# The ending of a fused state-space and attention kernel: when all engines branch on a flag, and where the flag is made

## The chip, the cores and the metric

The kernel runs on one core of a Trainium2 chip. The metric is the device time of one execution in microseconds (us).

## The reference

The input is `A_x`, 2048 rows of 1024 numbers in bf16. Two results are computed from it and mixed by a gate:

```python
g = _sigmoid((x * gate_w).sum(-1, keepdims=True))
# a: a diagonal state-space model with complex states
h = Lam_bar[None, :] * h + Bu[:, t, :]            # for each of 2048 steps t
y = 2.0 * jnp.einsum("blp,dp->bld", hseq, Cmat).real + x * Dskip[None, None, :]
# b: attention with 32 heads of 32 columns
scores = jnp.einsum("bhqd,bhkd->bhqk", q, k) * (Dh ** -0.5)
p = _softmax(scores, axis=-1)
o = jnp.einsum("bhqk,bhkd->bhqd", p, v)           # then reshaped, @ wo
return g * a + (1 - g) * b
```

The output has 2048 rows of 1024 bf16 numbers.

## The kernel before

The program holds two complete versions of the computation. The fast one assumes that the sums of the softmax lie in a safe range. It counts, at its end, whether all of them did, and makes a flag of the count. If the flag is zero, the program is done. Otherwise the general version, whose code follows, computes everything again. With the inputs of this case the flag is zero.

The fast version's attention runs in 512 bursts; a burst is two blocks of 128 keys, four heads and 256 queries. In each, PE forms scores (L1625), ACT takes their exponential (L1644, L1641), and PE multiplies by the values (L1728). The projections, the state-space model and the output matrix fill the gaps in portions that a planner places. The output is made in 16 tiles of 128 rows; each tile is collected in a buffer in SBUF (`fin`, which shares its memory with `f_xT` and so bears that name in the profile) and stored by one DMA of 256 KB that SP issues (`st_out`, L1573).

A small scheduler, `Sched`, keeps one list of operations for each engine (`pe`, `act`, `dve`, `pool`, `sp`). It works out from declared reads and writes which semaphores an operation waits for. All engines run their lists in order. `force_signal` makes an operation raise its engine's semaphore though no other operation in the lists needs it.

The last two tiles, 14 and 15, are finished in `tail`. For each of them (index `r`) PE multiplies the last group of attention results by the last rows of `wo`, once for each half of the columns (L2023, two matmuls for each `r`, into banks `2 + r` and `4 + r`). The first half is then copied by ACT (L2032), the second half added up by DVE (L2036), and `st_out` stores the tile. DVE has meanwhile reduced the checks to one bit per partition, `badb` (L2017). A matmul with a single column adds these up in bank 7 (L2026), and DVE converts the sum to an integer in SBUF, `flag` (L2034). In the kernel before, that matmul stands between the matmuls of tile 14 and tile 15, and the conversion ahead of DVE's part of tile 14.

After its list each engine runs the code of `stream`. It waits for the flag's conversion (L2092), loads the flag into a register (L2094, TENSOR_LOAD in the profile) and branches on it (L2095, COMPARE_BRANCH). A location for a branch hint is marked some way ahead in each list (`MARK_AT` operations before its end) and tied to this branch. The block of all engines is closed by a DRAIN on each and a barrier by semaphores (they bear L2060 in the profile).

`final_waits` waits for the semaphores of the DMA lanes: with `late` False for all lanes but those of the last two DMAs, with `late` True for the lanes of the last two, the stores of tiles 14 and 15. In the kernel before SP alone calls it: with False ahead of the flag, with True behind the branch.

Of the kernel before, what the change touches and what calls it, by code (L numbers as in the profile page):

```python
# [960 lines left out]
class FastPath:  # L961
# [85 lines left out]
    def dve(self, fn, r, w, name=""):  # L1047
        return self.S.op("dve", fn, reads=r, writes=w, name=name)
# [927 lines left out]
    def tail(self):  # L1976

        S, ps, OT, wo, dve = self.S, self.ps, self.OT, self.wo, self.dve
        chk, rc, osum = self.chk, self.rc, self.osum
        z = self.ut[:, 1, 0:34]  # L1980
        dve(lambda e: e.memset(z, 0.0), [], ["z"] + [("ut", 1)])

        def check(u0, u1, s0, s1, c):

            ra = rc[:, u0:u1].rearrange("p u g -> p (u g)")
            t, z2 = self.ut[:, 0, 0:8 * (u1 - u0)], self.ut[:, 1, 128:128 + s1 - s0]
            rcs, oss = [("rc", u) for u in range(u0, u1)], [("os", u) for u in range(s0, s1)]
            dve(lambda e: e.tensor_scalar(t, ra, RC_MAX, None, ALU.is_le), rcs, [("ut", 0)])
            dve(lambda e: e.scalar_tensor_tensor(t, ra, RC_MIN, t, ALU.is_ge, ALU.mult, accum_out=chk[:, c:c + 1]), rcs + [("ut", 0)], [("ut", 0), ("chk", c)])
            dve(lambda e: e.scalar_tensor_tensor(z2, osum[:, s0:s1], 0.0, z[:, s0:s1], ALU.mult, ALU.is_equal, accum_out=chk[:, c + 1:c + 2]), oss + ["z"], ["z2", ("chk", c + 1)])  # L1990

        def preload(r):
            for n in range(2):
                S.op("pe", lambda e, r=r, n=n: e.matmul(ps[:, 2 + r, :], self.ident[:], self.hilo[2 * r][n], start=(n == 0), stop=False),
                     reads=["ident", ("hi", 2 * r), ("lo", 2 * r)], name="preload", writes=[("tb", 2 + r)] + ([("S", 1)] if r == n == 0 else []), **({} if r == n == 0 else dict(acc=[("S", 1)])))
        assert self.os_n == 32 and not self.bg2
        check(0, 63, 0, 32, 0)
        self.pv(4 * NBURST - 8, 4 * NBURST - 4)
        preload(0)
        self.pv(4 * NBURST - 4, 4 * NBURST - 2)  # L2000
        self.pv(4 * NBURST - 2, 4 * NBURST)
        preload(1)
        ov = ps[:, 6, 0:264].rearrange("p (a c) -> p a c", a=8)
        On = self.On[:, 1]
        dve(lambda e: e.reciprocal(rc[:, 63], ov[:, :, 32]), ["O"], [("rc", 63)], "rcp")
        for t in range(2):
            o = On[:, t].rearrange("p (h c) -> p h c", h=4)
            dve(lambda e, t=t, o=o: e.scalar_tensor_tensor(o, ov[:, 4 * t:4 * t + 4, 0:32], self.gcol[:, 1, 14 + t:15 + t],
                                                           rc[:, 63, 4 * t:4 * t + 4].unsqueeze(2).to_broadcast([128, 4, 32]), ALU.mult, ALU.mult,
                                                           accum_out=osum[:, 32 + t:33 + t]), ["O", ("rc", 63), "g1"], [("On", 1, t), ("os", 32 + t)], "norm")  # L2010
            S.op("pe", lambda e, t=t: e.matmul(ps[:, t, 0:128], On[:, t], self.ident[:], start=True, stop=True),
                 reads=[("On", 1, t), "ident"], name="xp", **(dict(writes=[("S", 0), ("xp", t)]) if t == 0 else dict(acc=[("S", 0)], writes=[("xp", t)])))
        for t in range(2):
            self.act(lambda e, t=t: e.activation(OT[:, 7, 1792 + 128 * t:1920 + 128 * t], ps[:, t, 0:128], ACT.Copy), [("xp", t)], [("OT", 7, 7, t)], "xp")
        check(63, 64, 32, 34, 2)
        dve(lambda e: e.tensor_reduce(chk[:, 4:5], chk[:, 0:4], AX.X, ALU.add), [("chk", c) for c in range(4)], [("chk", 4)])
        dve(lambda e: e.tensor_scalar(self.badb[:, 0:1], chk[:, 4:5], 545.5, None, ALU.is_lt), [("chk", 4)], ["badb"])  # L2017

        for r in range(2):
            for cb in range(2):  # L2020
                bank = 2 + r + 2 * cb
                w = dict(acc=[("tb", bank)]) if cb == 0 else dict(writes=[("tb", bank)] + ([("S", 2)] if r == 0 else []), **({} if r == 0 else dict(acc=[("S", 2)])))
                S.op("pe", lambda e, r=r, cb=cb, bank=bank: e.matmul(ps[:, bank, :], OT[:, 7, 1792 + 128 * r:1920 + 128 * r], wo[7][0][:, 512 * cb:512 * (cb + 1)],  # L2023
                                                                    start=(cb == 1), stop=True), reads=[("OT", 7, 7, r), "wo7"], name="tail", **w)
            if r == 0:
                S.op("pe", lambda e: e.matmul(ps[0:1, 7, 0:1], self.badb[:, 0:1], self.badb[:, 1:2], start=True, stop=True), reads=["badb", "one"],  # L2026
                     writes=[("bank", 7)], name="flag")
        for r in range(2):
            fb = self.fin_n % 8 // 2
            self.fin_n += 2  # L2030
            o = self.fin[fb]
            self.act(lambda e, o=o, r=r: e.activation(o[:, 0:512], ps[:, 2 + r, :], ACT.Copy), [("tb", 2 + r)], [("fin", fb, 0)], "evac_t")  # L2032
            if r == 0:
                self.flag_op = dve(lambda e: e.tensor_copy(self.flag[:], ps[0:1, 7, 0:1]), [("bank", 7)], ["flag"], "flag")  # L2034
                self.flag_op.force_signal = True
            dve(lambda e, o=o, r=r: e.scalar_tensor_tensor(o[:, 512:1024], ps[:, 4 + r, :], 1.0, self.sum7[2 * r + 1], ALU.mult, ALU.add),  # L2036
                [("tb", 4 + r), ("sum7", 2 * r + 1)], [("fin", fb, 1)], "evac_t")
            self.st_out(14 + r, fb)
def bass_gated_mix__ssm_conv_s5__mha_block__prompt_kernel(
    nc: bass.Bass,  # L2040
    A_x: bass.AP,
# [18 lines left out]
    with ExitStack() as es:  # L2060
        S = Sched(n_dma_lanes=15, own=1)
        S2 = Sched(n_dma_lanes=12, pool_in_order=True, serial_xpose=True)
        sems = {l: es.enter_context(nc.semaphore("f_" + l)) for l in S.lanes()}
        sems2 = {l: es.enter_context(nc.semaphore("g_" + l)) for l in S2.lanes()}
        go = es.enter_context(nc.semaphore("go"))
        flag = es.enter_context(nc.sbuf_tensor("flag", [1, 1], I32))
# [14 lines left out]
        def stream(name, e):  # L2081

            loc = []
            S.emit(name, e, sems, MARK_AT[name], lambda: loc.append(e.mark_branch_hint_location()))
            if not loc:
                loc.append(e.mark_branch_hint_location())
            if name == "pool":
                for _ in range(272):
                    e.nop()
            if name == "sp":  # L2090
                S.final_waits(e, sems, False)
            e.wait_ge(sems[fast.flag_op.lane], fast.flag_op.tick)  # L2092
            with e.register("bad_" + name) as r:
                e.reg_load(r, flag[0:1, 0:1])  # L2094
                br = e.br_cmp(r, 0, on_true="done_" + name, on_false="bad_" + name, comp_op="IS_EQ")  # L2095
                br.branch_hint(loc[0])
                with e.bass.body("bad_" + name):
                    if name == "sp":
                        S.final_waits(e, sems, True)
                        e.nop().then_inc(go, 1)  # L2100
                    e.wait_ge(go, 1)
                    S2.emit(name, e, sems2)
                    if name == "sp":
                        S2.final_waits(e, sems2)
                    e.br("done_" + name)
                e.bass.switch_bb("done_" + name)
            if name == "sp":
                S.final_waits(e, sems, True)

        @block.sync  # L2110
        def _(e):
            stream("sp", e)

        @block.tensor
        def _(e):
            stream("pe", e)

        @block.vector
        def _(e):
            stream("dve", e)  # L2120
# [36 lines left out]
```

## Time and profile before

| | |
|---|---|
| median of 3 runs | 925.74 us (924.91 to 925.8) |
| profiled execution | 925.63 us |
| its span, first to last instruction | 923.9 us |
| PE busy | 901.5 us (98%) |
| ACT busy | 905.7 us (98%) |
| DVE busy | 770.5 us (83%) |
| SP's stores of the output | 16, median 2.2 us from issue to landing |

Busy times are shares of the span. An engine's name with a q (SPq, DVEq) stands for its sequencer, whose instructions (waits, register loads, branches, the issue of DMAs) are not counted as busy. Of the DMA queues, q1 carries the data that SP and ACT ask for; q8 and q14 carry instructions, in packets of 16 KB and 8 KB. The median from issue to landing counts from the start of the issuing instruction to the last update of the DMA's semaphore. The ending that the change touches is the stretch from about 917 us to the end of the span.

### The profile page before, as it was taken

How to read it: one execution, taken by the hardware profiler on the slowest of the kernel's cores; microseconds unless marked ns; L12 is line 12 of the kernel's file. 1: busy time of each engine (PE TensorE's matmuls, PEld its weight loads, DVE VectorE, ACT ScalarE, POOL GpSimd, SP SyncE). 2: the span in 40 equal slices, each digit the busy share in tenths (PEclk: the TensorE clock that was granted, in tenths of full speed). 3: DMA queues.
4: the chain of work that ended last, by engine and by line, in shares of the span. 5: the costliest groups of instructions: out<-in, count | busy, mean ns of one | idle time of the engine just before them, and what ended most of it. 6: DMA issues, size and time to landing. Idle time of an engine off the chain costs nothing.

```text
span 923.9 us, 34036 instructions
## 1 busy us (share of the span) xinstructions
PE 901.5 (98%) x15316; PEld 503.1 (54%) x15316; DVE 770.5 (83%) x1345; ACT 905.7 (98%) x1034; POOL 86.4 (9%) x163
## 2 busy tenths in 40 slices
PE   8899999999999999999999999999999999999996
PEld 4555744556555565555655565555655655545553
DVE  2788989999989999999999999989998655676665
ACT  6999999999999999999999999999999999999996
POOL 2000001011000101010111110101001010000010
PEclk9999999999999999999999999999999999999999
DMA  9449767630564202242212621622001012534422
GB/s 199 86 101 150 105 116 146 139 83 16 104 118 100 65 20 72 75 97 53 41 41 77 127 50 25 133 65 67 20 22 48 21 60 69 185 85 129 114 62 75
DMA packets 170983, 77.70 MB, mean 84 GB/s; under 512 B 147280, under 2 KB 155472, under 8 KB 170832
## 3 DMA queue, kind: packets, MB, share of 16 engines
q1 hardware_dynamic: 168672, 74.94, 35.7%
q8 instruction: 121, 1.98, 0.9%
q10 hardware_dynamic: 2160, 0.53, 0.3%
q14 instruction: 30, 0.25, 0.1%
HBM read 25.18 MB, written 20.97 MB: 50 GB/s over the span
## 4 chain that ended last, share of the span: by engine, by line
PE 54%; ACT 36%; DVE 5%; SPq 1%; DMA 1%; issue 1%; POOL 0%; DVEq 0%
ACT f_pt L1644 29%; PE f_ps L1728 14%; PE f_ps L1625 11%; PE f_ps L1427 9%; PE f_ps L1505 8%; PE f_ps L1458 6%; PE f_ps L1446 5%; ACT f_pt L1641 5%; SPq L1063 1%; ACT f_cT L1644 1%; DVE f_ht L1363 1%; ACT f_Et L1644 1%; PE f_ps L1707 1%; DMA f_xT<-in_A_x_dram 1%; PE f_ps L1511 0%
## 5 line engine op out<-in xcount | busy, mean ns | idle before, releaser
L1644 ACT ACTIVATE f_pt<-f_ps 128x1024 bf16<-128x1024 f32 x746 | 718.2, 1086 | 2.7 <-PE f_ps L1625 2.3
L1728 PEld LDWEIGHTS f_ps<-f_V,f_pt 128*128 128x128 bf16 x7156 | 220.8, 96 | 96.1 <-issue 69.7
L1728 PE MATMUL f_ps<-f_V,f_pt 128*128 128x33 bf16 x7156 | 257.2, 178 | 0.6 <-ACT f_pt L1644 0.6
L1625 PE MATMUL f_ps<-f_Q,f_K 32*128 32x256 bf16 x4096 | 203.3, 273 | 9.0 <-ACT f_cT L1644 2.2
L1641 ACT ACTIVATE f_pt<-f_ps 128x768 bf16<-128x768 f32 x198 | 176.6, 892 | 0.0
L1625 PEld LDWEIGHTS f_ps<-f_Q,f_K 32*128 32x128 bf16 x4096 | 60.7, 92 | 146.8 <-ACT f_pt L1644 118.5
L1458 PE MATMUL f_ps<-f_xT,f_wb 128*128 128x512 bf16 x512 | 131.5, 379 | 1.3 <-DVE f_pf L1240 0.5
L1666 POOL TENSOR_SCALAR f_xp<-f_xq 128x512 int16<-128x512 f32 x99 | 66.9, 676 | 618.9 <-DVE f_xq L1665 418.5
L1427 PE MATMUL f_ps<-f_xT,f_wb 128*128 128x512 bf16 x464 | 119.3, 379 | 0.4 <-DVE f_Q L1434 0.3
L1634 DVE TENSOR_SCALAR f_xi<-f_ps 128x256 int32<-128x256 f32 x198 | 83.4, 421 | 15.9 <-PE f_ps L1625 11.6
L1363 DVE TENSOR_TENSOR_SCAN f_ht<-f_pf,f_init,f_ut 128x512 bf16<-128x512 f32 x64 | 81.1, 1279 | 0.0
L1505 PE MATMUL f_ps<-f_cT,f_hp 128*128 128x512 bf16 x272 | 74.5, 379 | 0.1
L1669 DVE SCALAR_TENSOR_TENSOR f_xq<-f_xq,f_xi 128x512 f32<-128x512 f32 x99 | 68.5, 692 | 3.3
L1668 DVE SCALAR_TENSOR_TENSOR f_xq<-f_xi 128x512 f32<-128x512 uint16 x99 | 68.5, 692 | 3.3
L1665 DVE SCALAR_TENSOR_TENSOR f_xq<-f_xi,f_xq 128x512 f32<-128x512 int16 x99 | 68.2, 689 | 2.2
L1458 PEld LDWEIGHTS f_ps<-f_xT,f_wb 128*128 128x128 bf16 x512 | 40.1, 96 | 40.3 <-issue 9.1
L1446 PE MATMUL f_ps<-f_wb,f_xT 128*128 128x128 bf16 x896 | 59.3, 219 | 0.0
L1427 PEld LDWEIGHTS f_ps<-f_xT,f_wb 128*128 128x128 bf16 x464 | 36.1, 96 | 35.9 <-issue 7.6
L1446 PEld LDWEIGHTS f_ps<-f_wb,f_xT 128*128 128x128 bf16 x896 | 50.4, 97 | 3.8 <-issue 3.8
L1462 DVE CAST f_ub<-f_ps 128x512 bf16<-128x512 f32 x64 | 44.0, 688 | 9.5 <-PE f_ps L1458 8.6
L1741 DVE RECIPROCAL f_rc<-f_ps 128x8 f32<-128x8 f32 x63 | 13.0, 207 | 40.0 <-PE f_ps L1707 34.5
L1536 PE MATMUL f_ps<-f_cT,f_OT 128*128 128x512 bf16 x156 | 44.7, 378 | 0.1
(149 smaller groups left out, 829.0 us busy)
## 6 DMA issues: line engine op xcount, KB each, us to landing
u_scratch<-f_ub SPq DMA_DIRECT2D x64, 128.0 KB, 2.0
f_ub<-u_scratch SPq DMA_DIRECT2D x32, 256.0 KB, 2.9
ag_scratch<-f_Ag SPq DMA_DIRECT2D x32, 256.0 KB, 2.2
f_hp<-ag_scratch SPq DMA_DIRECT2D x32, 256.0 KB, 3.0
f_wb<-in_B_wqkv_dram SPq DMA_DIRECT2D x21, 256.0 KB, 4.1
out_dram<-f_xT SPq DMA_DIRECT2D x16, 256.0 KB, 2.2
f_cT<-in_B_wo_dram SPq DMA_DIRECT2D x5, 256.0 KB, 5.5
f_OT<-f_On SPq DMA_TRANSPOSE x63, 2.5
```

What stands on the lines that cost most here:

```text
L1363: ops.append((1.2, 0.0, lambda ri=ri: dve(lambda e: e.tensor_tensor_scan(ht[:, ri, :], rr, ut[:, ri, :], self.init[:, ri, j:j + 1], ALU.mu ...
L1427: mms.append((1, lambda e, f, l, a=a, w=w: e.matmul(ps[:, bank, :], w[:, a, :], xT[:, a, 512 * ch:512 * (ch + 1)], start=f, stop=l), [tok] ...
L1446: m = e.matmul(ps[:, bank, 128 * q:128 * (q + 1)], xT[:, a, 128 * kt:128 * (kt + 1)], w[:, a, :], start=(a == 0), stop=(a == 7))
L1458: mms.append((1, lambda e, f, l, a=a: e.matmul(ps[:, 7, :], bT[:, (2 * n + ri) % 3, a, :], xT[:, a, 512 * ch:512 * (ch + 1)], start=f, sto ...
L1505: mms.append((1, lambda e, f, l, j=j, ri=ri, h=h: e.matmul(ps[:, 7, :], h[:, cols], cT[ri][:, j, 512 * cb:512 * (cb + 1)], start=f, stop=l ...
L1625: m = e.matmul(ps[:, 2 * sl[h // 2] + h % 2, 256 * kl:256 * (kl + 1)], K[32 * h:32 * h + 32, g % 2, 128 * kt:128 * (kt + 1)], Q[32 * h:32 ...
L1634: first = self.dve(lambda e: e.tensor_scalar(self.xi[:, b % 2, X_COLS * n:X_COLS * (n + 1)], ps[:, 2 * s + 1, 512 - X_COLS:512], X_A, X_LO ...
L1641: self.S.op("act", lambda e: e.activation(flat(self.tile[p]), flat(ps[:, 2 * s:2 * s + 2, :]), ACT.Exp, scale=SCALE), reads=[("S", s)], wr ...
L1644: self.act(lambda e: e.activation(self.tile[p], ps[:, 2 * s:2 * s + 2, :], ACT.Exp, scale=SCALE), [("S", s)], [("pt", p)], "exp")
L1668: return [(0.61, DEP, lambda: self.dve(lambda e: e.scalar_tensor_tensor(xq[:], lo, E2 / E3 * w, lo, ALU.add, ALU.mult), i2, ["xq"], "x_q") ...
L1669: (0.61, DEP, lambda: self.dve(lambda e: e.scalar_tensor_tensor(xq[:], xq[:], E1 / E3 * w * w, lo, ALU.add, ALU.mult), ["xq"] + i2, ["xq"] ...
L1728: m = e.matmul(ps[:, 6, o:o + 33], self.tile[p][:, h2, 256 * kl + 128 * qt:256 * kl + 128 * (qt + 1)], V[:, g % 2, 2 * i + kl, h, :], star ...
```

## The change

In `tail`, the flag's matmul moves behind all four matmuls of tiles 14 and 15, and its conversion on DVE moves behind both of DVE's evictions and the issue of both stores in program order. In `stream`, every engine now waits for the last two stores between the load of the flag and the branch; SP no longer does so after the branch, nor does the code of the general version.

```diff
@@ tail
-            if r == 0:
-                S.op("pe", lambda e: e.matmul(ps[0:1, 7, 0:1], self.badb[:, 0:1], self.badb[:, 1:2], start=True, stop=True), reads=["badb", "one"],
-                     writes=[("bank", 7)], name="flag")
+        S.op("pe", lambda e: e.matmul(ps[0:1, 7, 0:1], self.badb[:, 0:1], self.badb[:, 1:2], start=True, stop=True), reads=["badb", "one"],
+             writes=[("bank", 7)], name="flag")
         for r in range(2):
...
             self.act(lambda e, o=o, r=r: e.activation(o[:, 0:512], ps[:, 2 + r, :], ACT.Copy), [("tb", 2 + r)], [("fin", fb, 0)], "evac_t")
-            if r == 0:
-                self.flag_op = dve(lambda e: e.tensor_copy(self.flag[:], ps[0:1, 7, 0:1]), [("bank", 7)], ["flag"], "flag")
-                self.flag_op.force_signal = True
             dve(lambda e, o=o, r=r: e.scalar_tensor_tensor(o[:, 512:1024], ps[:, 4 + r, :], 1.0, self.sum7[2 * r + 1], ALU.mult, ALU.add),
                 [("tb", 4 + r), ("sum7", 2 * r + 1)], [("fin", fb, 1)], "evac_t")
             self.st_out(14 + r, fb)
+        self.flag_op = dve(lambda e: e.tensor_copy(self.flag[:], ps[0:1, 7, 0:1]), [("bank", 7)], ["flag"], "flag")
+        self.flag_op.force_signal = True
@@ stream
             e.wait_ge(sems[fast.flag_op.lane], fast.flag_op.tick)
             with e.register("bad_" + name) as r:
                 e.reg_load(r, flag[0:1, 0:1])
+                S.final_waits(e, sems, True)
                 br = e.br_cmp(r, 0, on_true="done_" + name, on_false="bad_" + name, comp_op="IS_EQ")
                 br.branch_hint(loc[0])
                 with e.bass.body("bad_" + name):
                     if name == "sp":
-                        S.final_waits(e, sems, True)
                         e.nop().then_inc(go, 1)
...
                 e.bass.switch_bb("done_" + name)
-            if name == "sp":
-                S.final_waits(e, sems, True)
```

## The prediction

> **What bounds the kernel now.** The change touches only what comes after the last evictions, so I read the page for the span and then only the last seven microseconds, in this order: the timeline, SP's waits, the DMA traffic by queue, and the lines of the branch and of the closing barrier.
>
> ```profile
> span 923.9 us, 34036 instructions
> ```
>
> The profiled execution took 925.63 us, so 1.73 us lie outside its span. The median of the three runs is 925.74 us, 0.11 above it; I make the sum against the profiled execution and add 0.11 at the end.
>
> The timeline of the ending (start, length, engine, line, operation):
>
> ```profile
> 916.40 0.55 ACT L2014 ACTIVATE f_OT<-f_ps 128x128 bf16<-128x128 f32 x2 [1.39 <-PE f_ps L2011]
> ...
> 916.74 0.61 PE L2023 MATMUL f_ps<-f_cT,f_OT 128*128 128x512 bf16 x2
> ...
> 916.95 0.16 DVE L2017 TENSOR_SCALAR f_badb<-f_chk 128x1 bf16<-128x1 f32 x1
> 917.16 1.23 ACT L2032 ACTIVATE f_xT<-f_ps 128x512 bf16<-128x512 f32 x2 [0.21 <-PE f_ps L2023]
> ...
> 917.27 0.17 PE L2026 MATMUL f_ps<-f_badb 128*1 128x1 bf16 x1
> ...
> 917.37 0.61 PE L2023 MATMUL f_ps<-f_cT,f_OT 128*128 128x512 bf16 x2
> 917.47 0.14 DVE L2034 CAST flag<-f_ps 1x1 int32<-1x1 f32 x1 [0.36 <-PE f_ps L2026]
> 917.55 1.27 DVE L2036 SCALAR_TENSOR_TENSOR f_xT<-f_ps,f_Et 128x512 bf16<-128x512 f32 x2
> ```
>
> SP's own timeline and its waits (engine and line, for what, us in total, times, longest):
>
> ```profile
> 918.30 0.92 SPq L1573 DMA_DIRECT2D out_dram<-f_xT  x2
> ...
> SPq L195 <- DMA out_dram<-f_xT: 2.3, 1, 2.3
> SPq L2060 <- DMA out_dram<-f_xT: 0.6, 1, 0.6
> ```
>
> The last computation ends at 917.55 + 1.27 = 918.82; the span ends at 923.9. The five microseconds between are SP alone, standing in front of the last two stores. So this ending is bounded by the landing of the stores, and the question is why that takes so long. The DMA view of 918 to 924 (queue: packets, MB, share of 16 engines; then the issue, KB, median us to landing), and below it the instruction queues' lines of three shorter windows, 919 to 920.2, 920.2 to 920.6 and 921.4 to 921.6:
>
> ```profile
> q1 hardware_dynamic: 288, 0.52, 26.2%
> q14 instruction: 4, 0.03, 2.2%
> q8 instruction: 1, 0.02, 1.0%
> ...
> out_dram<-f_xT SPq DMA_DIRECT2D x2, 256.0 KB, 4.6
> ...
> q14 instruction: 3, 0.02, 7.9%
> ...
> q8 instruction: 1, 0.02, 15.5%
> ...
> q14 instruction: 1, 0.01, 17.8%
> ```
>
> Both last stores need 4.6 us. The page's median over all 16 stores, the store of 907.4 (DMA view of 907 to 910, without an instruction queue in it), and the store of 872.9 (872.8 to 876.7, with one instruction packet in it):
>
> ```profile
> out_dram<-f_xT SPq DMA_DIRECT2D x16, 256.0 KB, 2.2
> ...
> q1 hardware_dynamic: 144, 0.26, 23.4%
> ...
> out_dram<-f_xT SPq DMA_DIRECT2D x1, 256.0 KB, 2.0
> ...
> q8 instruction: 1, 0.02, 2.3%
> ...
> out_dram<-f_xT SPq DMA_DIRECT2D x1, 256.0 KB, 3.7
> ```
>
> An undisturbed store lands in 2.0 to 2.2 us; one that shares its time with an instruction fetch takes 3.7; the last two share theirs with five fetches and take 4.6. Where the five fetches come from is read from the branch (L2095), the flag's loads into registers (L2094) and the closing barrier (L2060): duration in ns, then the start.
>
> ```profile
> L2094 DVEq TENSOR_LOAD <-flag x1: 546/546/546, 918.0 to 918.0; - x1
> L2094 SPq TENSOR_LOAD <-flag x1: 762/762/762, 919.6 to 919.6; - x1
> ...
> L2095 POOLq COMPARE_BRANCH  x1: 65/65/65, 918.2 to 918.2; - x1
> L2095 PEldq COMPARE_BRANCH  x1: 496/496/496, 918.2 to 918.2; - x1
> L2095 ACTq COMPARE_BRANCH  x1: 68/68/68, 918.3 to 918.3; - x1
> L2095 DVEq COMPARE_BRANCH  x1: 84/84/84, 918.6 to 918.6; - x1
> L2095 SPq COMPARE_BRANCH  x1: 78/78/78, 920.4 to 920.4; - x1
> ...
> L2060 POOLq DRAIN  x1: 125/125/125, 918.6 to 918.6; - x1
> L2060 PEldq DRAIN  x1: 58/58/58, 918.8 to 918.8; - x1
> L2060 ACTq DRAIN  x1: 78/78/78, 918.8 to 918.8; - x1
> L2060 DVEq DRAIN  x1: 34/34/34, 919.2 to 919.2; - x1
> L2060 SPq COMPARE_BRANCH  x1: 53/53/53, 923.5 to 923.5; - x1
> L2060 SPq DRAIN  x1: 13/13/13, 923.7 to 923.7; - x1
> ```
>
> Five engines branch and five instruction packets move: four branches between 918.2 and 918.6, four packets between 919 and 920.6; SP's branch at 920.4, and a lone packet in 921.4 to 921.6, some 1.1 us behind it. I take it that each taken branch makes its engine fetch more code, and that these fetches fall on the DMA engines that carry the stores issued at 918.30 and 918.89. No view shows the DMA engine of a packet, so the collision itself is inferred.
>
> **The change part by part.** *The flag leaves the head of the evictions.* The conversion at 917.47 stands ahead of the first DVE eviction, and waits for a matmul that waits for L2017's result. The bank that the eviction reads is done at 916.74 + 0.61 = 917.35. The DVE took up the flag 0.03 us after its matmul's end at 917.44; by the same step the eviction starts at 917.38 instead of 917.55, 0.17 earlier. The second follows: it starts 1.27 - 0.67 = 0.60 later, at 917.98 (0.67 being half of the pair's work, about 1.3 us). Its bank is ready before that: tile 15's operand is there at 916.40 + 0.55 = 916.95, matmuls of this kind follow at 0.61 - 0.38 = 0.23 us, and without the flag's matmul between them the second pair runs from 917.19 to 917.80. The ACT evictions, 917.16 to 918.39, end before the DVE's. So the DVE ends at 918.65 and the last store is issued at 918.72. Gain 0.17, bounds 0 and 0.2.
>
> *The flag itself.* It is now made after 918.65, so at about 918.82. Four engines then load it in some 0.55 us (the DVE's row) and are done at 919.4. SP gets there after its store: its load of 919.6 to 920.4 moves up by the 0.17 to end at 920.2. All this lies beside the stores. It would cost something only if they landed before 920.2, 1.5 us after the last issue, and none did so in under 2.0.
>
> *The waits for the stores, on all five engines.* Behind them on each engine stand the branch, the drain and the barrier, and nothing else; only the barrier waits for these. The waits cost nothing before the landing.
>
> *The fetches move behind the landing.* With every branch behind both stores, no branch-made fetch can disturb them. The landing goes from 4.6 to between 2.0 (alone, 907.4) and 2.4: the two stores are 0.59 us apart, and 0.52 MB in the way makes the second one queue a little. I take 2.2, the page's median: 918.72 + 2.2 = 920.92, against 918.89 + 4.6 = 923.5 before. If the fetches are not the cause, this gain of 2.4 is nil.
>
> *The branch is now exposed.* Before, SP alone came late and had only its jump left: 923.5 to the DRAIN's end at 923.7, 0.2 us. Now all five branch at 920.94. From the start of the branch to the end of the drain it was 0.5 us on POOL, 0.66 on PE, 0.58 on ACT and 0.63 on DVE. I take 0.65 for the latest, with 0.5 and 0.9 as bounds. That is a loss of 0.45. The barrier after it stays: 923.9 - 923.7 = 0.2.
>
> The sum: 920.94 + 0.65 + 0.2 = 921.8 for the span, against 923.9, or -0.17 - 2.4 + 0.45 = -2.1. With the 1.73 outside, 923.5; with 0.11 for the median, **923.6 us**, 0.23% less.
>
> **A rule that speaks against it.** The four drains start between 918.6 and 919.2, and four of the five fetches had not arrived by 919.2: the code behind the branch was already there, and the fetches were for later code. The Trainium skill, page "Runtime: NRT & Kernel Launch", section "Instruction fetch mechanics", says that a taken branch whose target is outside the two pages at hand stops its engine until that page has been fetched. Here the trace shows no such stop. Where the rule bites, the fetch would stand behind the landing on all five engines, which is the third rival below, at 926.4 us; by the row of the drains it does not, and the sum stays.
>
> **The rivals.** *The fetches become the tail.* The code fetched after the branch may be needed soon after the barrier, in the part outside the span. Today there are three microseconds of landing to hide it. SP's packet moved 1.1 us after its branch; PE's, branched at 918.2, moved from 920.2 to 920.6 at the earliest and took 1.0% of 16 engines' 6 us, about 1 us, so its code was there 3.0 to 3.4 us after the branch. From 920.94 that makes 922.6 (1.1, and half a microsecond for a packet of q14: 2.2% of 16 engines' 6 us, by four) to 924.3, and with the 0.2 and 1.73 a time of 924.5 to 926.2, likeliest 925.1. For it speaks that each engine did fetch; against it, that no drain or barrier waited for a fetch.
>
> *The stores land late for another reason.* Being two in a row, say. Then the landing stays 4.6: 918.72 + 4.6 + 0.65 + 0.2 = 924.2, so 925.9 to 926.0, no change. Against it speaks the single store at 872.9 with 3.7. Equivalent to it is that the fetches come by the clock of the code stream and not by the branch; SP's lone packet after its lone branch speaks against that.
>
> *The prefetched target is lost while the engines stand in front of the branch.* Then each must fetch its target first: 3.0 to 3.4 us by PE's case, 920.94 + 3.4 + 0.06 + 0.2 = 924.6, so 926.4, slower than before; if the line after the target must also come, twice that, near 929.8. It is slower than before from a stop of 2.6 us on, and by over 0.2% from some 4.5 us. Against it: the targets were fetched long before the branch in the run of before and survived.
>
> **How the numbers follow.** 0.2% of this time is 1.85 us, about what a measurement can tell from no change. The forecast gets 0.70; by its own bounds (2.0 to 2.4 for the landing, 0.5 to 0.9 for the branch) it reaches from 923.2 to 924.1, and most of that, 0.64, is faster by over 0.2%, 0.06 within. The exposed fetch gets 0.14 and the other reason 0.07, both within 0.2%. The lost target gets 0.09, of which 0.07 is slower by over 0.2%. That is 0.64, 0.29 and 0.07. The range goes from 922.8 (the lower bound, less the scatter of the three runs) to 925.7, which takes in most of the exposed fetches and leaves out the rest.
>
> **What would show it.** Right: both last stores landing in about 2.2 us; no instruction packet until some 1.1 us behind the branches; the flag's conversion last on DVE; the first L2036 at 917.4 on this clock; five branches at nearly one time, and 0.65 us from there to the last drain; a span near 921.8. Wrong: landings still above 4 us, drains over 1 us behind the branches, or a time that falls less than the span does, which would be code missing after the end.

## The result and the profile after

| | before | after |
|---|---|---|
| median, 22 runs each | 925.45 us | 923.95 us |
| ratio after / before | | 0.9984, 95% interval 0.9978 to 0.9990 |
| profiled execution | 925.63 us | 923.51 us |
| its span | 923.9 us | 921.8 us |

The change made the kernel 0.16% faster. That is inside the stated range (922.8 to 925.7) and 0.35 us above the forecast of 923.6. The forecast was 2.1 us (0.23%) below the median of before as it then stood, 925.74; the medians moved by 1.5, the two profiled executions by 2.1.

DVE's, ACT's, PE's and SP's timelines of the changed kernel's ending, then SP's waits (the lines have moved: L2031 and L2032 are the evictions, L2025 and L2035 the flag's matmul and conversion):

```profile
917.35 1.29 DVE L2032 SCALAR_TENSOR_TENSOR f_xT<-f_ps,f_Et 128x512 bf16<-128x512 f32 x2 [0.33 <-PE f_ps L2023]
918.56 0.13 DVE L2035 CAST flag<-f_ps 1x1 int32<-1x1 f32 x1
...
917.13 1.08 ACT L2031 ACTIVATE f_xT<-f_ps 128x512 bf16<-128x512 f32 x2 [0.27 <-PE f_ps L2023]
...
916.71 1.04 PE L2023 MATMUL f_ps<-f_cT,f_OT 128*128 128x512 bf16 x4 [0.15 <-ACT f_OT L2014]
917.67 0.16 PE L2025 MATMUL f_ps<-f_badb 128*1 128x1 bf16 x1
...
918.12 0.92 SPq L1573 DMA_DIRECT2D out_dram<-f_xT  x2
...
SPq L2094 <- DMA out_dram<-f_xT: 0.6, 1, 0.6
```

The four matmuls now run without a break, DVE's evictions start at 917.35 and end at 918.64, and the flag comes last. The last store is issued at 918.71 instead of 918.89. The DMA view of 916.5 to 921.9, and, under it, the instruction queues of 921.9 to 924:

```profile
q1 hardware_dynamic: 288, 0.52, 26.0%
...
out_dram<-f_xT SPq DMA_DIRECT2D x2, 256.0 KB, 2.2
...
q14 instruction: 4, 0.03, 4.5%
q8 instruction: 1, 0.02, 3.1%
```

The same 288 packets of the two stores move, no instruction packet among them. The 2.2 us of this view is the second store's alone, against 4.6 before; the last update of the first store's semaphore comes at 920.15, 2.0 us after its issue. (q1 carries SP's transfers only: ACT's two loads of 256 KB and five of 2 KB at the start of the kernel are the 0.53 MB of q10.) The five instruction packets are still there, but behind the end of the span. The branches (L2094), the register loads (L2092) and the closing drains (L2058), duration in ns and start:

```profile
L2092 ACTq TENSOR_LOAD <-flag x1: 757/757/757, 918.7 to 918.7; - x1
L2092 DVEq TENSOR_LOAD <-flag x1: 822/822/822, 918.7 to 918.7; - x1
L2092 SPq TENSOR_LOAD <-flag x1: 746/746/746, 919.5 to 919.5; - x1
...
L2094 SPq COMPARE_BRANCH  x1: 73/73/73, 920.9 to 920.9; - x1
L2094 POOLq COMPARE_BRANCH  x1: 65/65/65, 920.9 to 920.9; - x1
L2094 DVEq COMPARE_BRANCH  x1: 84/84/84, 920.9 to 920.9; - x1
L2094 PEldq COMPARE_BRANCH  x1: 500/500/500, 920.9 to 920.9; - x1
...
L2058 POOLq DRAIN  x1: 127/127/127, 921.4 to 921.4; - x1
L2058 SPq DRAIN  x1: 61/61/61, 921.4 to 921.4; - x1
L2058 DVEq DRAIN  x1: 36/36/36, 921.5 to 921.5; - x1
```

All branches start together behind the landing; the last drain, DVE's, ends 0.66 us after its branch, and the span 0.2 to 0.3 us after that.

### The profile page after: what moved, and what is told of

Read it like the earlier page. It is cut to its first block, busy times and chain, and to the rows that moved or that the text cites. A ratio compares the mean times of both kernels' runs of the same rounds, so it can differ in the third digit from the quotient of the medians.

```text
span 921.8 us, 33819 instructions
## 1 busy us (share of the span) xinstructions
PE 882.5 (96%) x15095; PEld 503.1 (55%) x15316; DVE 770.5 (84%) x1345; ACT 905.5 (98%) x1034; POOL 86.3 (9%) x163
## 4 chain that ended last, share of the span: by engine, by line
PE 48%; ACT 36%; DVE 10%; issue 2%; SPq 1%; DMA 1%; POOL 0%
ACT f_pt L1644 29%; PE f_ps L1728 12%; PE f_ps L1625 10%; PE f_ps L1427 8%; PE f_ps L1505 7%; ACT f_pt L1641 5%; PE f_ps L1446 5%; PE f_ps L1458 5%; DVE f_xi L1634 2%; DVE f_ht L1363 2%; SPq L1063 1%; ACT f_cT L1644 1%; ACT f_Et L1644 1%; PE f_ps L1707 1%; DVE f_Ag L1518 1%
## 5 line engine op out<-in xcount | busy, mean ns | idle before, releaser
L1458 PE MATMUL f_ps<-f_xT,f_wb 128*128 128x512 bf16 x448 | 117.7, 379 | 8.0 <-DVE f_xi L1634 1.2
L1427 PE MATMUL f_ps<-f_xT,f_wb 128*128 128x512 bf16 x406 | 106.7, 379 | 4.9 <-DVE f_Q L1434 0.5
L1505 PE MATMUL f_ps<-f_cT,f_hp 128*128 128x512 bf16 x240 | 67.6, 379 | 2.6 <-DVE f_Ag L1518 0.3
L1354 DVE TENSOR_TENSOR f_ut<-f_ht,f_tq 128x512 f32<-128x512 bf16 x64 | 42.2, 686 | 0.7
```

The source lines that it names most:

```text
L1427: mms.append((1, lambda e, f, l, a=a, w=w: e.matmul(ps[:, bank, :], w[:, a, :], xT[:, a, 512 * ch:512 * (ch + 1)], start=f, stop=l), [tok] ...
L1458: mms.append((1, lambda e, f, l, a=a: e.matmul(ps[:, 7, :], bT[:, (2 * n + ri) % 3, a, :], xT[:, a, 512 * ch:512 * (ch + 1)], start=f, sto ...
L1505: mms.append((1, lambda e, f, l, j=j, ri=ri, h=h: e.matmul(ps[:, 7, :], h[:, cols], cT[ri][:, j, 512 * cb:512 * (cb + 1)], start=f, stop=l ...
```

## The experiments

The stretch ahead of the ending varies between executions by more than the effects in question (ACT's first eviction starts between 917.1 and 918.7 us in the profiles). So besides each time I use the *ending*: from the start of ACT's first eviction in the timeline to the end of the span, in one profile. Before it is 923.9 - 917.16 = 6.7 us, after 921.8 - 917.13 = 4.7. The theory under test: the branches make the engines fetch code, the fetches disturb the stores, and the gain comes from keeping them apart. The main rival: something else delays the last stores, and the wait, or the flag's place, cures that.

**The late flag alone.** The edit takes the tail of the change and the old `stream`:

```diff
 # tail: as in the change
 # stream: as before
                 e.reg_load(r, flag[0:1, 0:1])
-                S.final_waits(e, sems, True)
                 br = e.br_cmp(r, 0, on_true="done_" + name, on_false="bad_" + name, comp_op="IS_EQ")
...
+            if name == "sp":
+                S.final_waits(e, sems, True)
```

> The flag is made behind the last evictions, as in the change, but nobody waits for the stores ahead of the branch. Theory (fetches made by the branches disturb the stores): the flag is ready at 918.7, four engines have loaded it by 919.5 and branch, their fetches start 1.1 us later, at 920.6, when the stores' packets are over (920.5 in the changed kernel); both stores land in at most 2.3 us, and SP has only its jump left behind the landing (0.2 instead of 0.65 us), so the span is 921.3, shorter than that of the whole change (921.8), and the time 923.0 to 923.3. Rival (the stores land late unless all engines stand still): landings over 4 us, span near 923.5, time near 925.3.

Measured: 923.58 us against 926.35 of the kernel before on that chip, ratio 0.997 (0.996 to 0.9981). The span, ACT's eviction, and the DMA view of 919.6 to 921.9 of this kernel, with the instruction queue's line of the next half microsecond below, and its branches and drains:

```profile
span 922.8 us, 34037 instructions
...
918.62 1.08 ACT L2031 ACTIVATE f_xT<-f_ps 128x512 bf16<-128x512 f32 x2 [0.21 <-PE f_ps L2023]
...
q1 hardware_dynamic: 284, 0.52, 61.1%
...
out_dram<-f_xT SPq DMA_DIRECT2D x2, 256.0 KB, 2.1
...
q14 instruction: 3, 0.02, 16.8%
...
L2093 ACTq COMPARE_BRANCH  x1: 68/68/68, 921.0 to 921.0; - x1
L2093 DVEq COMPARE_BRANCH  x1: 84/84/84, 921.1 to 921.1; - x1
L2058 SPq COMPARE_BRANCH  x1: 53/53/53, 922.4 to 922.4; - x1
L2058 SPq DRAIN  x1: 13/13/13, 922.5 to 922.5; - x1
```

Four engines branch at 921.0 to 921.1, more than a microsecond ahead of the last landing at 922.4, and the stores still land in 2.1 us: the fetches start after 921.9, when 284 of the stores' 288 packets have started (by the trace's packet records the last of the 288 ends at 921.96 and the first fetch starts at 922.12). So nobody has to stand still; the fetches only have to come late enough. SP has its jump alone behind the landing, and the ending is 4.2 us, half a microsecond shorter than that of the whole change.

**The waits alone.** The change's `stream` with the old tail:

```diff
                 e.reg_load(r, flag[0:1, 0:1])
+                S.final_waits(e, sems, True)
                 br = e.br_cmp(r, 0, on_true="done_" + name, on_false="bad_" + name, comp_op="IS_EQ")
 # tail: as before, flag ahead of the first eviction on DVE
```

> The waits of the change alone: all engines wait for both stores ahead of the branch, but the flag is made where it was, ahead of the first eviction on DVE. Theory: landings of 2.2 us as in the changed kernel, the last store issued 0.17 us later (918.88 instead of 918.71), so a span of 922.0 and a time 0.17 us above that of the whole change, 924.1. Rival (the place of the flag is what makes the gain): landings over 4 us, time near 925.3.

Measured: 924.82 against 926.35, ratio 0.9984 (0.9975 to 0.9993); landings of 2.0 and 2.1 us; an ending of 922.8 - 918.07 = 4.7, which does not resolve the 0.17 expected over the whole change's. The place of the flag is thus no condition for the gain; either edit alone keeps fetches and stores apart. The 924.1 of the expectation, like the absolute times of the expectations before and behind it, was for the first chip; on this one the kernel before is 0.9 us slower, and the ratio is the one to compare.

**A wait for the first store only.**

```diff
                 e.reg_load(r, flag[0:1, 0:1])
+                S.final_waits(e, sems, True, 1)      # lane of tile 14's store only
                 br = e.br_cmp(r, 0, on_true="done_" + name, on_false="bad_" + name, comp_op="IS_EQ")
 # behind the branch: SP waits for both, as before; tail: as in the change
```

> The flag is late as in the change, and all engines wait ahead of the branch for the first of the two stores only (landed at 920.15 in the changed kernel); SP alone waits for the second, behind its branch. Theory: branches at 920.2, fetches from 921.3, no collision; four engines have drained at 920.85, and SP goes from the second landing (920.87) through its jump (0.2) and the barrier (0.2): span 921.3, time 923.0 to 923.3. If the fetched code is what the part outside the span waits for, that part shrinks too, from 1.86 to 1.73 us. Rival (the last store lands late when anything branches ahead of its landing): landing over 3 us, span over 922.

Measured: 924.26 against 926.35, ratio 0.9978 (0.9969 to 0.9987). Landings of 2.0 and 2.2, branches at 920.5 and 920.6, no instruction packet until 921.3, and an ending of 921.7 - 917.50 = 4.2 us, the same as with the late flag alone. The second store lands on time though everything branches ahead of its landing.

**One fetch put back, a small one.** Flag early, waits on all engines but POOL:

```diff
-                S.final_waits(e, sems, True)
+                if name != "pool":
+                    S.final_waits(e, sems, True)
 # tail: as before
```

> One fetch put back: the flag is early as before, four engines wait for both stores ahead of the branch, POOL alone branches at once (918.2). Theory: one instruction packet moves at 919.3, on one of 16 DMA engines, amid the stores; at least one store lands 0.8 to 1.6 us late (3.0 to 3.8 us in all, as the store with one fetch beside it in the trace of before), span 922.8 to 923.6, time 924.5 to 925.4. Rival (one small packet is nothing; it is SP's branch, or the sum of all five, that disturbs): landing 2.2, span 922.0, time 924.1.

Measured: 925.72 against 926.35, ratio 0.9991 (0.9982 to 1.0). The DMA view of 919.7 to 923.3, the landings of the two stores, and the branches of POOL and SP:

```profile
q1 hardware_dynamic: 288, 0.52, 39.2%
q14 instruction: 1, 0.01, 1.1%
...
DMA to landing us min/median/max: 2.6/2.8/2.9
...
L2097 POOLq COMPARE_BRANCH  x1: 65/65/65, 919.7 to 919.7; - x1
L2097 SPq COMPARE_BRANCH  x1: 73/73/73, 923.3 to 923.3; - x1
```

One branch, one instruction packet amid the stores, and both stores are late, by 0.6 and 0.8 us. The packet took 1.1% of 16 engines' 3.6 us, 0.6 us. The expectation of 3.0 to 3.8 was too high: it was taken from a store beside a 16 KB packet. The ending, 924.2 - 918.65 = 5.55 us, is 0.8 longer than the 4.73 of the waits alone. The time says the same beside the waits alone (925.72 against 924.82), but the interval against the kernel before reaches 1.0.

**One fetch put back, a large one.** The same with PE in POOL's place:

```diff
-                if name != "pool":
+                if name != "pe":
                     S.final_waits(e, sems, True)
```

> The size of the fetch: flag early, four engines wait for both stores ahead of the branch, PE alone branches at once, so that one packet of 16 KB (about 1.0 us) moves amid the stores instead of POOL's of 8 KB (0.6 us), which made the landings 2.6 and 2.9 us. Theory (a store is late by about the time that the fetch takes on the DMA engine they share): landings of 3.0 to 3.5 us, an ending of 5.7 to 6.1 us from ACT's first eviction to the end of the span (5.6 with POOL's). Rival (each fetch costs the same, whatever its size): 2.6 and 2.9 again. If PE's fetch starts over 2 us after its branch, as in the profile of before, it misses the stores: 2.0 and 2.15.

Measured: 926.35 against 926.38, ratio 1.0003 (0.9994 to 1.0012). The DMA view of 919.2 to 923.7 and the landings:

```profile
q1 hardware_dynamic: 288, 0.52, 32.0%
q8 instruction: 1, 0.02, 1.5%
...
DMA to landing us min/median/max: 2.3/3.1/3.9
```

The packet took 1.5% of 16 engines' 4.5 us, 1.1 us; the stores were late by 0.3 and 1.7 us, and the ending is 924.6 - 918.11 = 6.5. Both expectations missed: it is not a fixed price per fetch, and the second store lost more than the packet's own time. The single large fetch, with the exposed branch behind it, eats the whole gain.

No view names the DMA engine of a packet, but the trace's semaphore updates show where the delay falls. Each store's semaphore gets sixteen updates, one for each sixteenth of its packets (nine of the 144). Of the second store here fifteen came within 2.1 us of the issue, by 921.94, and one at 923.71. With POOL's fetch it was again fifteen in 2.1 us and one late. In the six profiles without a fetch amid the stores no sixteenth took over 2.2 us, and in two profiles of the kernel before twelve came in 2.1 us and four late, as many as the fetches of the four early branches. The DMA view of PE's run from 921.6 to 923.6, when the fifteen were through:

```profile
q1 hardware_dynamic: 9, 0.02, 3.3%
```

So one fetch holds up one sixteenth of a store and leaves the others alone. In the packet records the late sixteenth's nine packets start at 922.26, as the fetch ends, and run to 923.26, while the others were through at 921.57. Four packets of the first store just ahead of the fetch, which by their times stand in the same row, took 0.15 to 0.20 us each, and the first three behind it 0.17 to 0.23, where 0.08 is usual. These seven, with the fetch's own 1.07 us, make up about the 1.7 us; why they were slow is not shown.

**The kernel before, a second time**, unchanged:

> The kernel before, unchanged, for a second profile of its ending. From ACT's first eviction (L2032) to the end of the span it took 6.7 us in the first profile, with landings of 4.6 us. The changed kernel saved 2.1 us in its profile but only 1.5 in the medians. Theory A (the disturbance differs from execution to execution, and the first profile showed a strong one): landings here between 3 and 4.6 us, an ending of 5.6 to 6.7 us. Theory B (the disturbance is always the same, and the rest of the difference is scatter of the part ahead of the ending): landings of 4.6 again, an ending of 6.7.

Measured: 926.21 against 926.38 of its sister runs, ratio 0.9997 (0.9988 to 1.0006). Its span, ACT's eviction, its landings, and its first branch, SP's branch and its last drain:

```profile
span 924.7 us, 34036 instructions
...
918.53 1.23 ACT L2032 ACTIVATE f_xT<-f_ps 128x512 bf16<-128x512 f32 x2 [0.21 <-PE f_ps L2023]
...
DMA to landing us min/median/max: 4.0/4.1/4.2
...
L2095 POOLq COMPARE_BRANCH  x1: 65/65/65, 919.6 to 919.6; - x1
L2095 SPq COMPARE_BRANCH  x1: 78/78/78, 921.8 to 921.8; - x1
L2060 SPq DRAIN  x1: 13/13/13, 924.4 to 924.4; - x1
```

Theory A holds: the disturbance was weaker here, 4.0 and 4.2 us instead of 4.6, with the same five packets, and the ending 6.2 instead of 6.7.

**The whole change, and the late flag alone, a second time on one chip**, both unchanged:

> The changed kernel, unchanged, on the same chip as the kernel with the late flag alone. Theory: an ending of 4.6 us from ACT's first eviction to the end of the span as in its first profile, landings of 2.0 and 2.15; time 0.14% to 0.23% under the kernel before. If the fetched code is awaited after the end, its part outside the span is longer than that of the kernel before; if not, both are about 1.8 us.

> The late flag without any wait ahead of the branch, a second time, now beside the whole change. Theory: an ending of 4.15 us against 4.6, all of it SP's jump of 0.2 in place of the exposed branch and drain of 0.65, so 0.45 us or 0.05% faster than the whole change. Rival (the first comparison was right in size): 1 us or 0.1% faster than the whole change.

Measured, beside the same runs of the kernel before (926.38): the whole change 924.62, ratio 0.9981 (0.9972 to 0.999), the late flag alone 924.07, ratio 0.998 (0.9971 to 0.9989). Spans and ACT's evictions of the two:

```profile
917.78 1.08 ACT L2031 ACTIVATE f_xT<-f_ps 128x512 bf16<-128x512 f32 x2 [0.21 <-PE f_ps L2023]
...
span 921.5 us, 34037 instructions
...
917.36 1.08 ACT L2031 ACTIVATE f_xT<-f_ps 128x512 bf16<-128x512 f32 x2 [0.21 <-PE f_ps L2023]
```

The first of the three lines is the whole change, whose span was 922.4: an ending of 4.6, as in its first profile. The other two are the late flag alone: 4.1, as in its first profile within a tenth. The medians differ by 0.55 us, near the 0.45 expected, but the ratios by only 0.0001, and their intervals overlap, so the times alone do not prove the order, but the endings do not overlap. The late flag without any wait is thus the better version of the two in the endings, by half a microsecond, and it is no slower in any comparison.

Of these runs, what lies outside the span is 1.77 us for the whole change and 1.78 for the kernel before (medians over the runs). In the whole change's profile the last fetch ends 1.5 us behind the span, in the kernel before ahead of the span's end; so the fetches behind the span add nothing to the part outside it.

## Why the prediction was right

**The landing.** Forecast 4.6 to 2.2 us; the last store took 2.2, the one before it 2.0. The cause was inferred from five branches and five packets; the runs show it: no fetch amid the stores, landings of 2.0 to 2.2 in every profile; one, 2.6 to 2.9 or 2.3 to 3.9; five, 4.0 to 4.6. That the two stores in a row land late by themselves, the second rival, is refuted by the same runs, and so is its twin, that the fetches come by the clock of the code stream: they moved with the branches in every run. The collision itself, which the prediction could only infer, is the one late sixteenth for each fetch. The store of 872.9, beside which a load of 256 KB also ran, shows the same: fifteen updates in 2.0 us and one at 3.7.

**The head of the evictions.** Forecast 0.17 us earlier, first eviction at 917.38, last store at 918.72. It was 917.35 and 918.71; ACT's first eviction, at 917.13 against 917.16, shows 0.03 of that to be scatter of what came before.

**The exposed branch.** Forecast 0.65 us from the branches to the last drain; it was 0.66, DVE's. The prediction had read its four times from starts rounded to 0.1 us; unrounded they are 0.60 on POOL, 0.61 on PE, 0.56 on ACT and 0.66 on DVE, so the 0.5 that it took as the lower bound was misread, and the term itself hardly moves. SP's own path, which the trace of before could not show, is shorter (its drain ends at 921.47).

**The flag.** It stayed hidden, but the loads took 0.75 to 0.82 us on the other engines too, not the 0.55 taken from DVE's row; the four end at 919.5 and SP's at 920.2, still 0.6 us ahead of the landing.

**The lost target.** All drains end within 0.66 us of the branch, and the fetches behind them: waiting ahead of the branch lost nothing. The rule of the Trainium skill ("Runtime: NRT & Kernel Launch", "Instruction fetch mechanics") did not bite: DVE, which stood in front of its branch for over a microsecond, took 0.66 us from there to the end of its drain, and 0.66 in the kernel before, where it had not waited.

**The tail of fetches.** Refuted by the 1.77 and 1.78 us outside the span on one chip. (On the first chip the 22 runs of the changed kernel have 1.86, but there only one run of the kernel before has a span, with 1.73, so the two are not compared.)

**What was off.** The profiled executions moved by the 2.1 us of the sum, the medians by 1.5. The term most likely mis-sized as a typical value is the 4.6 us landing of before: a second profile of the same kernel, on another chip, has 4.0 for the last store, and with that the sum is -0.17 - 1.8 + 0.45 = -1.5 us. This is argued, not shown. The profiled executions stood 0.18 us above (before) and 0.44 below (after) the medians of their kernels, which is the whole difference of 0.6. The changed kernel's ending was alike in its two profiles, 4.7 and 4.6, so its 0.44 lay outside the ending; only if the stretch ahead of the ending is typically as long in both kernels does the difference fall on the landing of before. That the two profiles hit the sum to a tenth was therefore partly luck. How the landings spread over all runs was not measured; two profiles show only that they differ. The chance of 0.64 for more than 0.2% rested on that one profile; the interval of the first comparison, 0.10% to 0.22%, lies on both sides of the bound.

## What to carry to other kernels

When a store takes much longer than its like, look at which other queues moved packets in the same window, the instruction queues among them. A taken branch costs more than its own time: in these profiles its engine's instruction packet started 1.1 to 1.8 us later, PE's 1.2 to 2.2, and held up a store that was still moving. So place a branch where no transfer on the critical path is moving, here so late that the transfer's packets are already through. It need not wait for the landing itself, only for the data to have moved. And a stall that comes from a collision differs between executions; one profile shows that it is there, not its mean.

## What the hardware showed that was not expected

Loading the flag into a register took 0.48 to 0.55 us on four engines in the kernel before, mostly ahead of the first store's issue, and 0.75 to 0.82 us in the changed kernel, beside the stores; SP's load, beside the stores in both, took 0.76 and 0.75. An 8 KB instruction packet amid the stores made them 0.6 and 0.8 us late, a 16 KB packet 0.3 and 1.7, each time through a single one of a store's sixteen parts; with five packets, four of them small, the lateness was 1.9 to 2.5 us.
